# Four positions per partition for q and k, with f16 transposes by column tiles and strided queries, in a block-causal attention and expert kernel

## Chip, cores, metric

One core of one Trainium2 chip. The metric is the device time of one execution in microseconds; medians and the lowest and highest of the runs are given, over all runs, the slow ones of a kernel too (over 1.5% above its fastest); ratios use the fast ones alone. Executions of one kernel spread here (412.61 to 422.98 us for the nine runs of the kernel before on one chip), so small differences are judged by ratios with 95% intervals.

## The reference, cut to what matters

```python
B, H, S, D = 8, 8, 576, 64              # q, k, v: f32
scores = q @ k.T / sqrt(D)              # per batch and head
mask   = (pos_i // 64) >= (pos_j // 64) # causal by blocks of 64
attn   = softmax(where(mask, scores, -1e9))
x      = (attn @ v).transpose(0, 2, 1, 3).reshape(4608, 512)
# eight experts: each row of x goes to the expert that domain_id names
out[rows of e] = relu(x[rows of e] @ w1[e]) @ w2[e]    # 512 -> 1024 -> 512
```

The kernel works on 32 pairs of heads (8 batches of 4 pairs), then on the eight experts. Both halves are long; the change is in the first.

## The kernel before

The parts that matter. Staging and loads: q and k arrive as f32 with 128 consecutive positions on 128 partitions, so every run in memory is one head's 64 values, 256 B.

```python
qS = [asb.tile([128, 4, 16, D], F32, name=f"qS{i}") for i in range(2)]   # kS alike, tS for tails
def load_qk(i, b0, b1, h0=0, h1=H):
    ...
    for c in range(4):
        nc.gpsimd.dma_start(out=dst[t % 2][:, c, o, :],
                            in_=rows(src, i, b0, b1, h0, h1, c))
```

Transposes of one pair of heads, in f32, with one PSUM buffer and one copy that casts to f16:

```python
def emit_T(p):
    PT = aps.tile([128, 2, 512], F32, name="PT", tag="PT")
    QK = asb.tile([128, 2, 512], F16, name="QK", tag="QK", bufs=3)
    for s, src in enumerate((qS[t % 2], kS[t % 2])):
        for c in range(4):
            nc.tensor.transpose(out=PT[:, s, 128 * c : 128 * c + 128],
                                in_=pair_cols(src[:, c], p), identity=identf[:])
    nc.vector.tensor_copy(out=QK[:], in_=PT[:])
```

Products: the keys are the stationary operand, the queries the moving one, contiguous in QK; each of the two heads uses its own 64 rows of the array (64*128 in the views), and the two run beside each other: both 512-wide products together last 0.39 us at 47.40 us of the kernel before.

```python
def mm_qk(o, QK, c):
    for i in range(2):
        h = slice(64 * i, 64 * i + 64)
        nc.tensor.matmul(out=o[:, i], lhsT=QK[h, 1, 128 * c : 128 * c + 128],
                         rhs=QK[h, 0, 128 * c : 512], start=True, stop=True)
```

PV is the product of the attention weights with v. The order of work for pair p: group 0 (512-wide product), transposes of pair p+2, group 1 (384 + 128), the PV products of pair p-1, group 2 (256 and twelve 64-wide ones), the rest of PV. ScalarE takes the exponentials, VectorE copies out of PSUM and divides, GpSimd casts v to f16 and issues the loads.

The softmax here doesn't subtract the row's maximum and nothing guards it: scores larger than these inputs give would overflow.

## Time and profile before

| | before |
|---|---|
| time | 421.58 us median (417.69 to 422.23, 3 runs) |
| span of the profiled run | 415.3 us |
| last division of attention starts (with its reciprocal) | 189.6 us |
| first gather of the experts | 196.87 us |
| first gather to end | 218.4 us |

The page divides the span into 40 slices of 10.4 us. Each digit is a busy share in tenths, and PEclk is the clock granted to TensorE in tenths:

```profile
PE   2764841998989879881499999969979597799000
PEclk9995985789699968998589999997989899699655
```

The first 18 digits are attention. PE has holes until the fourteenth or so, and the clock falls in and after them (8.85 us busy and a mean clock of 0.57 from 60 to 80 us). Two groups of TensorE (line, engine, operation, output<-inputs, shape, count, then busy us, mean ns of one, and idle time before them with its cause):

```profile
L336 PE MATMUL ps<-QK 64*128 64x512 f16 (+3 forms) x256 | 37.5, 335 | 0.7 <-ACT ATE L341 0.7
L394 PE MATMUL po<-vS,A 128*128 128x65 f16 x640 | 36.6, 201 | 0.0
```

The mean of 335 ns mixes four widths; the 64x512 products alone have a mean of 428 ns.

### The profile page before, as it was taken

What the parts mean: (1) busy time and instruction counts of PE and PEld (TensorE: products, weight loads), DVE (VectorE), ACT (ScalarE), POOL (GpSimd) and SP (SyncE); (2) the same over time, 40 slices, a digit from 0 to 9 for tenths busy, and PEclk for the clock granted to TensorE, in tenths of its full rate; (3) what the DMA queues carried; (4) which work ended last, traced back from release to release, by engine and by line L of the source; (5) the groups of instructions that cost most, each with busy time, mean ns of one, the idle gap of its engine ahead of it and who ended that gap; (6) DMA issues with size and microseconds to landing.
All of it is one profiled execution on the core that took longest, in us unless ns stands there. A gap on an engine that the chain in (4) does not pass through costs nothing. (4 is left out here: it accounts for less than half of the span.)

```text
span 415.3 us, 6768 instructions
## 1 busy us (share of the span) xinstructions
PE 305.5 (74%) x2758; PEld 190.5 (46%) x2758; DVE 162.1 (39%) x268; ACT 140.7 (34%) x193; POOL 220.1 (53%) x253
## 2 busy tenths in 40 slices
PE   2764841998989879881499999969979597799000
PEld 1332620665666647661264656544636344365000
DVE  6641870659388746752204242222122221222000
ACT  1230730465468746790050504130503204032000
POOL 9999742875297400000787556474655755422220
PEclk9995985789699968998589999997989899699655
DMA  7799999999999991111289986949879496212120
GB/s 148 202 235 249 229 186 231 221 256 229 204 283 209 259 192 33 29 58 59 84 140 217 211 161 141 172 120 182 151 150 174 106 184 128 84 62 77 64 76 14
DMA packets 36097, 64.48 MB, mean 155 GB/s; under 512 B 9082, under 2 KB 21886, under 8 KB 36064
## 3 DMA queue, kind: packets, MB, share of 16 engines
q0 software_dynamic: 26256, 58.08, 64.1%
q1 hardware_dynamic: 7408, 5.35, 5.1%
q10 hardware_dynamic: 2400, 0.59, 0.7%
q8 instruction: 23, 0.38, 0.4%
q14 instruction: 10, 0.08, 0.1%
HBM read 67.15 MB, written 15.20 MB: 198 GB/s over the span
## 5 line engine op out<-in xcount | busy, mean ns | idle before, releaser
L341 ACT ACTIVATE A<-ps 128x1024 f16<-128x1024 f32 (+1 forms) x96 | 84.4, 883 | 86.5 <-PE ps L336 78.5
L542 ACT ACTIVATE hT<-ph 128x640 f16<-128x640 f32 x64 | 45.1, 704 | 144.3 <-PE ph L537 144.3
L556 POOL DMA_INDIRECT out_dram<-osb,tok x40 | 40.9, 1023 | 76.9 <-DMA out_dram<-osb,tok 30.1
L551 PE MATMUL po<-w2h,hT 128*128 128x512 f16 x320 | 77.0, 404 | 0.0
L512 POOL DMA_INDIRECT xg<-x_rows,tok x40 | 40.6, 1015 | 65.9 <-issue 60.2
L537 PE MATMUL ph<-xT,w1h 128*128 128x320 f16 x512 | 73.2, 304 | 0.2 <-DVE xT L526 0.2
L537 PEld LDWEIGHTS <-w1h 128*128 128x128 f16 x512 | 50.8, 99 | 22.4 <-issue 0.6
L555 DVE COPY osb<-po 128x512 f32<-128x512 f32 x40 | 27.7, 691 | 75.0 <-PE po L551 45.4
L313 DVE CAST QK<-PT 128x1024 f16<-128x1024 f32 x32 | 39.0, 1219 | 38.0 <-PE PT L310 37.2
L551 PEld LDWEIGHTS <-hT 128*128 128x128 f16 x320 | 32.9, 104 | 40.8 <-issue 8.7
L526 DVE COPY xT<-pt 128x512 f16<-128x512 f16 x40 | 16.4, 423 | 75.8 <-PE pt L523 74.9
L310 PE MATMUL PT<-identf,qS 128*128 128x128 f32 x128 | 25.6, 322 | 21.1 <-DMA qS<-in_q_dram 9.1
L310 PE MATMUL PT<-identf,kS 128*128 128x128 f32 x128 | 26.2, 321 | 19.3 <-DMA kS<-in_k_dram 19.3
L523 PE MATMUL pt<-identh,xg 128*128 128x128 f16 x160 | 17.6, 246 | 30.9 <-DMA xg<-x_rows,tok 28.9
L336 PE MATMUL ps<-QK 64*128 64x512 f16 (+3 forms) x256 | 37.5, 335 | 0.7 <-ACT ATE L341 0.7
L394 PE MATMUL po<-vS,A 128*128 128x65 f16 x640 | 36.6, 201 | 0.0
L389 PE MATMUL po<-VE,ATE 128*128 128x130 f16 x160 | 33.2, 234 | 1.8 <-DVE x L411 1.8
L394 PEld LDWEIGHTS <-A 128*128 128x128 f16 x640 | 32.1, 103 | 1.0 <-issue 1.0
L411 DVE TENSOR_TENSOR x<-po,rc 128x768 f16<-128x768 f32 x32 | 30.6, 958 | 4.0 <-DMA x_rows<-x 2.9
L310 PEld LDWEIGHTS PT<-identf,qS 128*128 128x128 f32 x128 | 15.6, 157 | 31.7 <-DVE QT L326 9.0
L136 POOL DMA_DIRECT2D w2h<-in_moe_w_dram x32 | 23.4, 752 | 10.8 <-DMA kS<-in_k_dram 7.0
L310 PEld LDWEIGHTS PT<-identf,kS 128*128 128x128 f32 x128 | 18.3, 162 | 23.0 <-DMA kS<-in_k_dram 23.0
(92 smaller groups left out, 285.6 us busy)
## 6 DMA issues: line engine op xcount, KB each, us to landing
w1h<-in_moe_w_dram POOLq DMA_DIRECT2D x32, 256.0 KB, 5.6
w2h<-in_moe_w_dram POOLq DMA_DIRECT2D x32, 256.0 KB, 6.0
vst<-in_v_dram POOLq DMA_DIRECT2D x12, 512.0 KB, 7.4
qS<-in_q_dram POOLq DMA_DIRECT2D x12, 512.0 KB, 12.3
kS<-in_k_dram POOLq DMA_DIRECT2D x12, 512.0 KB, 18.8
x_rows<-x SPq DMA_DIRECT2D x8, 512.0 KB, 8.9
vst<-in_v_dram POOLq DMA_DIRECT2D x11, 256.0 KB, 4.0
qS<-in_q_dram POOLq DMA_DIRECT2D x4, 256.0 KB, 5.1
```

Source lines behind the costliest of these rows:

```text
L310: nc.tensor.transpose(out=PT[:, s, 128 * c : 128 * c + 128], in_=pair_cols(src[:, c], p), identity=identf[:])
L313: nc.vector.tensor_copy(out=QK[:], in_=PT[:])
L336: nc.tensor.matmul(out=o[:, i], lhsT=QK[h, 1, 128 * c : 128 * c + 128], rhs=QK[h, 0, 128 * c : 512], start=True, stop=True)
L341: nc.scalar.activation(out=o, in_=i, func=AF.Exp, scale=0.125)
L389: nc.tensor.matmul(out=o[:, 1:131], lhsT=st["AE"][:, 128 * m : 128 * m + 128], rhs=VE[b % 2][:, m, hp, 1:131], start=True, stop=(m == 0))
L394: nc.tensor.matmul(out=o[:, 1 + 65 * i : 66 + 65 * i], lhsT=at_block(st, i, c, m), rhs=vS[b % 3][:, c, hp, 1 + 65 * i : 66 + 65 * i], star ...
L411: nc.vector.tensor_tensor(out=st["x"][:, :, 128 * hp : 128 * hp + 128].rearrange("p (b w) (i z) -> p b w i z", b=2, i=2), in0=pv[:, :, :, ...
L512: nc.gpsimd.indirect_dma_start(out=g[:, blk, :], out_offset=None, in_=xd, in_offset=bass.IndirectOffsetOnAxis(ap=tok[:, blk : blk + 1], ax ...
L537: nc.tensor.matmul(out=ph[:, i, 0:hw], lhsT=w1h[:, dc, 128 * fc : 128 * fc + 128], rhs=xT[:, dc, hw * i : hw * i + hw], start=(dc == 0), s ...
L542: nc.scalar.activation(out=hT[:, fc].rearrange("p (i n) -> p i n", i=2), in_=ph[:, :, 0:hw], func=AF.Relu)
L551: nc.tensor.matmul(out=po[:], lhsT=hT[:, fc, 128 * blk : 128 * blk + 128], rhs=w2h[:, fc, :], start=(fc == 0), stop=(fc == 7))
L556: nc.gpsimd.indirect_dma_start(out=out, out_offset=bass.IndirectOffsetOnAxis(ap=tok[:, blk : blk + 1], axis=0), in_=osb[:], in_offset=None ...
```

## The change

The intent: longer runs for the loads of q and k, so that they take less DMA time. Each partition takes four neighbouring positions of one head, 1 KB in one run. Two consequences follow. First, a transpose now yields the positions in the order 0, 4, 8, ... for each of four offsets, so the keys are put in order by the copy out of PSUM, while the queries stay as they are and are read with a step. Second, the f32 staging is cast to f16 by GpSimd ahead of the transposes. The two heads of a pair no longer lie side by side, so each head is transposed into its own half of the array's columns (a column tile; 128*64 in the views below). The diff, cut to its core:

```diff
-    qS = [asb.tile([128, 4, 16, D], F32, name=f"qS{i}") for i in range(2)]
+    qs = asb.tile([128, 16, 256], F32, name="qs")          # ks alike
+    qh = [asb.tile([128, H, 256], F16, name=f"qh{i}") for i in range(4)]
 ...
+        eng.dma_start(
+            out=dst[:, o, :],
+            in_=src[b0:b1, h0:h1, n0 : n0 + 512, :].rearrange(
+                "b h (p j) d -> p (b h) (j d)", j=4))
 ...
     def emit_T(p):
-        PT = aps.tile([128, 2, 512], F32, name="PT", tag="PT")
+        PT = aps.tile([128, 2, 4, 128], F16, name="PT", tag="PT", bufs=2)
-            for c in range(4):
-                nc.tensor.transpose(out=PT[:, s, 128 * c : 128 * c + 128], ...)
-        nc.vector.tensor_copy(out=QK[:], in_=PT[:])
+            for j in range(4):
+                for i in range(2):
+                    nc.tensor.transpose(
+                        out=PT[64 * i : 64 * i + 64, s, j, :],
+                        in_=src[:, 2 * hp + i, 64 * j : 64 * j + 64],
+                        identity=identh[:])
+        nc.vector.tensor_copy(
+            out=QK[:, 0].rearrange("p (j n) -> p j n", j=4), in_=PT[:, 0])
+        nc.vector.tensor_copy(
+            out=QK[:, 1].rearrange("p (n j) -> p n j", j=4),
+            in_=PT[:, 1].rearrange("p j n -> p n j"))
+    def q_cols(QK, h, n0, n1):
+        return QK[h, 0].rearrange("p (j n) -> p n j", j=4)[:, n0 // 4 : n1 // 4, :]
 ...
-                rhs=QK[h, 0, 128 * c : 512], start=True, stop=True)
+                rhs=q_cols(QK, h, 128 * c, 512), start=True, stop=True)
```

Cut: the same reading of queries in the 64-wide products, the tails in f16, casts placed among the loads, a third buffer for gathered rows, and a clamped index for the gather.

## The prediction

> **What bounds the kernel now.** I split the span by stage first, then read who waits for whom, then the timeline of one pair of heads. The span has two halves: attention to about 190 us (the last division on VectorE starts at 189.83) and the experts from the first gather at 196.87 us. The change edits the experts hardly at all, so I ask what attention is worth. In stages of 20 us (columns: stretch, length, busy PE, PEld, DVE, ACT, POOL with counts, granted clock, DMA share, GB/s):
>
> ```profile
> 60.00:80.00 20.00, 8.85 (x90) 5.58 (x92) 5.06 (x6) 3.85 (x5) 8.67 (x11) 0.57 1.11 221
> 120.00:140.00 20.00, 17.72 (x275) 13.02 (x276) 15.31 (x21) 15.11 (x21) 14.48 (x16) 1.00 1.05 238
> 160.00:180.00 20.00, 18.85 (x298) 13.83 (x296) 15.98 (x22) 16.32 (x23) 0.00 (x0) 1.00 0.10 32
> ```
>
> From 20 to 155 us the DMA share is about 1 and TensorE has holes, with the clock halved after long ones; from 160 us the inputs are in and TensorE runs through. The table of waits names the holes:
>
> ```profile
> ACT A L341 <- PE ps L336: 78.5, 41, 16.7
> DVE QK L313 <- PE PT L310: 37.2, 12, 12.7
> PEld PT L310 <- DMA kS<-in_k_dram: 23.0, 13, 4.4
> PE PT L310 <- DMA qS<-in_q_dram: 9.1, 5, 5.1
> ```
>
> The transposes wait for k and q, and everyone else waits for TensorE. So attention is bound by the DMA until 155 us and by TensorE after. In single microseconds, v alone moves at about 340 GB/s, and q and k, with the same 256 B runs, at about 220:
>
> ```profile
> 120.00:121.00 1.00, 0.28 (x3) 0.28 (x4) 0.79 (x3) 0.92 (x1) 1.00 (x2) 1.00 1.09 360
> 129.00:130.00 1.00, 1.00 (x23) 0.70 (x19) 1.00 (x1) 0.70 (x1) 0.40 (x1) 1.00 1.10 229
> ```
>
> An unhindered pair has no hole on TensorE (timeline; start, length, then the group):
>
> ```profile
> 47.40 0.39 PE L336 MATMUL ps<-QK 64*128 64x512 f16 x2
> 47.72 0.66 PE L310 MATMUL PT<-identf,qS 128*128 128x128 f32 x4
> 48.21 0.60 PE L310 MATMUL PT<-identf,kS 128*128 128x128 f32 x4
> 48.74 0.39 PE L336 MATMUL ps<-QK 64*128 64x384 f16 x4
> ...
> 49.70 0.28 PE L336 MATMUL ps<-QK 64*128 64x256 f16 x2
> ```
>
> The next pair starts at 50.69, so a pair costs 3.29 us: transposes 1.02 (47.72 to 48.74), QK products 0.32 + 0.32 + 0.22 plus 0.31 for the twelve 64-wide ones, together 1.17, and 1.10 for PV. ACT needs 2 x 1.026 + 0.597 + 0.485 = 3.13 us a pair, so it stands just behind. 32 pairs at 3.3 are 106 us; attention takes 190. Some 65 us could be had.
>
> [...]the query operand becomes strided, and the kernel before has one such matmul to test it on, the routing product (L214, 120 moving columns, 36 B apart):
>
> ```profile
> L214 PE MATMUL PT<-Hh,L x36: 377/399/405, 80.5 to 105.5; 128*128 128x120 f16 x36
> 80.53 4.11 PE L214 MATMUL PT<-Hh,L 128*128 128x120 f16 x18
> ```
>
> Eighteen start within 4.11 us: (4.11 - 0.40)/17 = 0.218 us each, or 1.8 ns a column. Contiguous f16 runs at 0.053 us for 128 columns (eight expert transposes in 0.71 us), 0.42 ns a column. [...]the clock is 1.00 when L214 starts and 0.50 in the microsecond after its end.[...]
>
> **The change part by part.**
> 1. *Loads.* q and k are 18.9 MB. At 210 to 220 GB/s they cost about 88 us of the queue. If 1 KB runs reach the rate of v, 340 GB/s, it is 55 us: 33 us of DMA time removed. v keeps its runs (9.4 MB, 28 us). The DMA share adds up to about 148 us of full work before 156 us (135 from 20 to 155, the rest earlier); x and the first weights are what remains, about 32. The total falls to about 115 us. GpSimd issues one transfer instead of four.
> 2. *GpSimd casts.* 128x1024 f32 to f16 takes 1.045 us (the v casts). Per batch four such for q and k, and a half one: about 4.8 us, 34 us for seven batches, and fewer issues free about 35 us (48.8 us for the 50 issues of q, k and tails now, against 16 of about 1 us). GpSimd is idle from 145 to 197 us now, so this lies beside other work. Staging is now single, but each load can be issued right after its cast; I laid these out with the times above and find each batch ready 4 us or more before a slow TensorE wants it.
> 3. *Transposes.* Eight f32 ones (1.02 us) become sixteen f16 ones of 128 moving columns, 0.053 each: 0.85 us in series, 0.45 if two column tiles overlap. Gain 0.2 to 0.6 us.
> 4. *Evacuation.* One 1.219 us copy becomes a contiguous f16 one (0.42, as the 128x512 expert copies) and a reordering one of 512 elements (0.68[...], as the f32 tail copy, perhaps more). About even. PT has two buffers, which removes the short waits for QT and QK (about 1.2 us a batch, 10 us in all).
> 5. *Strided queries.* A pair has 512 + 384 + 128 + 256 = 1280 columns for QK and five 64-wide products more, 1600 columns with a step of 256 B between neighbours. At 1.8 ns that is 2.9 us in place of 1.15: **plus 1.75 us a pair**, on TensorE, which sets the pace once DMA doesn't.
>
> The sum: a pair costs 3.29 - 1.17 + 2.93 - 1.02 + 0.85 = 4.9 us (4.5 if column tiles overlap). From pair 2 at about 25 us, 30 pairs at 4.5 to 4.9 are 135 to 147 us, plus 8 for L214, 3 for the tails and 2 to drain: attention ends at 173 to 185 us, not 190. The 65 us of holes go, and 50 of them come back as slow reads. Experts unchanged (the gather now clamps its index; some 10% more rows): 421 - 5 to - 17 gives **404 to 416 us**.
>
> **Rivals.** *(a) The strided read costs little.* For it: [...]the author left the queries unordered while reordering the keys.[...] Then ACT at 3.13 and TensorE at about 3.2 us a pair set the pace, with some waits for casts in the first half; attention ends at 145 to 160 us and the kernel takes 375 to 392. I give this 0.25. *(b) The clock falls too.* Per pair the array is really fed for about 1600 x 0.42 = 0.67 us plus 0.81 us of PV columns in 4.9 us, 30%; L214 at 24% lost the clock, and the last pairs at about 50% (clock 1.00 at 184 to 190 us) did not. At half clock[...] 6 us a pair, attention to 215 or 225 us, total 440 to 455. I give this 0.27. *(c) A new wait on GpSimd*: casts behind issues in one queue, with one staging buffer. [...]batch 2 can come late; worth 5 to 10 us, and only if TensorE is fast.
>
> **Range and chances.** The middle case (0.48) puts two thirds of its weight below 413 us, the 2% line. With rival a: 0.25 + 0.48 x 0.6 = 0.54 faster; 0.20 same; 0.26 slower. Middle 409 us, range 378 to 447.
>
> **What would show it.** Mean length of the 64x512 QK matmul: 428 ns now; about 1100 if step 5 holds, 430 if rival a. The pair period in the middle of attention: 4.5 to 4.9, 3.2 or 6 us. DMA share below 0.8 from 60 us on, and few waits of the transposes for loads. Clock in attention: 1.0, or 0.5 for rival b. Sixteen transposes within 0.45 to 0.9 us. First gather at 180 to 192 us. The prediction is wrong [...]if two row tiles no longer overlap when strided, or if the late casts leave new holes.

Marks show where passages are cut from the recorded text: general statements about the hardware that no trace of this case shows, and reasons that rested on them. The sum of the middle case has all its terms: 3.29 - 1.17 + 2.93 - 1.02 + 0.85 = 4.88 us, put as 4.9 us a pair (4.5 if column tiles overlap), attention to 173 to 185 us, and 404 to 416 us in all. The 2.93 rests on L214's measured 1.8 ns a column; that a rate seen at a step of 36 B holds for the queries' 256 B was the author's estimate, and so were the rate of v for 1 KB runs and the full clock for such a pair. Rival b loses the clause from which its 6 us a pair came: 4.5 us, with PV's 1.10 and the overlapping transposes' 0.45 counted once more. No trace showed such growth, so it was an estimate too (the growth measured is in the last part but one).

## The result

The changed kernel takes 452.87 us (451.20 to 454.37, 3 runs) against 421.58 us. The ratio is 1.077, with a 95% interval of 1.065 to 1.089: slower, and outside the predicted range of 378 to 447. (A ratio here is the mean time of one kernel's fast runs over that of the other's of the same rounds, so not quite the ratio of the medians quoted.) The last division of attention starts at 223.6 us instead of 189.6, and the first gather is at 229.13 instead of 196.87. From there to the end it is 220.1 us against 218.4 (of the profiled runs). So nearly all of the loss lies in attention.

The two later stages of 20 us of the prediction, of the kernel after:

```profile
120.00:140.00 20.00, 20.00 (x205) 10.92 (x202) 8.54 (x16) 10.02 (x14) 11.79 (x15) 1.00 1.04 231
160.00:180.00 20.00, 20.00 (x211) 11.48 (x207) 7.92 (x16) 9.85 (x14) 0.00 (x0) 1.00 0.01 2
```

The holes are gone: PE is busy 20.00 of 20 us. But from 120 us on it finishes 205 matmuls where the kernel before finished 275, although each pair now has 16 transposes instead of 8. The DMA is idle from 160 us on. From the table of waits (who, for whom, total us, count, longest):

```profile
DVE rc L418 <- PE po L397: 84.5, 31, 3.7
```

VectorE waits for TensorE, as ScalarE does with 75.2 us for the products. From 80 to 220 us attention is bound by TensorE alone (20.00 of 20 us busy in each stage). One pair on its timeline (start, length, then the group):

```profile
112.11 1.02 PE L341 MATMUL ps<-QK 64*128 64x512 f16 x2
113.06 0.64 PE L311 MATMUL PT<-identh,qh 128*64 128x128 f16 x8
113.48 0.64 PE L311 MATMUL PT<-identh,kh 128*64 128x128 f16 x8
114.06 1.03 PE L341 MATMUL ps<-QK 64*128 64x384 f16 x4
115.02 0.29 PE L397 MATMUL po<-VE,ATE 128*128 128x130 f16 x1
...
115.32 0.43 PE L402 MATMUL po<-vS,A 128*128 128x65 f16 x4
...
115.65 0.54 PE L402 MATMUL po<-vS,A 128*128 128x65 f16 x6
116.12 0.60 PE L341 MATMUL ps<-QK 64*128 64x256 f16 x2
```

The divisions of neighbouring pairs of one batch are 6.0 us apart (112.2, 118.2). From starts, this pair has 0.95 for the 512-wide products, 1.00 for the transposes, 0.96 for the 384- and 128-wide ones, 1.10 us for the first part of PV, and about 1.25 for the 256- and 64-wide ones. The rest of PV takes 0.78 in the pair before it (111.33 to 112.11), which has no transposes of tails after it. **PV takes 1.88 us where it took 1.10 (0.64 and 0.46 in the pair of the prediction), and nothing was changed in it.** The groups agree:

```profile
L402 PE MATMUL po<-vS,A 128*128 128x65 f16 x640 | 55.4, 248 | 0.0
...
L311 PE MATMUL PT<-identh,kh 128*64 128x128 f16 x256 | 20.5, 314 | 2.6 <-POOL kh L112 2.6
```

The row of L341 has 84.3 us and a mean of 703 ns, more than twice the 335 of before (64x512 alone: 1021 ns). The transposes last 314 ns each and wait 2.6 us in all for GpSimd's casts of k (a like row has 8.2 us for VectorE's casts of q, at the start), and those of the tails 4.1 us.

The page, though, reports full clock for the whole of attention:

```profile
PE   2879969999999999999718999897978969699300
PEclk9999999999999999999999999999896959989855
```

That row can't be read so. The trace's first clock record is at 241.7 us, after attention, and it says "full". Before the first record the page assumes full clock. A first record that changes the clock *to* full means that it was not full before, and the durations confirm it: the PV groups last 0.29, 0.43 and 0.54 us, as in the kernel before where its records say half (0.29, 0.43, 0.54 from 39.77 to 40.40 us), against 0.23, 0.28 and 0.34 us where they say full (49.06 to 49.43). The clock was at half for all of attention. The reader should take from this that the clock row is only as good as its records; an unchanged matmul is the better thermometer.

### The profile page after: what moved, and what is told of

It is laid out like the page before. It is cut to its first block, busy times and chain, and to the rows that moved or that the text cites. A ratio compares the mean times of both kernels' runs of the same rounds, so it can differ in the third digit from the quotient of the medians.

```text
span 449.2 us, 7273 instructions
## 1 busy us (share of the span) xinstructions
PE 370.9 (83%) x3014; PEld 210.1 (47%) x3014; DVE 158.3 (35%) x302; ACT 144.8 (32%) x196; POOL 220.0 (49%) x252
## 5 line engine op out<-in xcount | busy, mean ns | idle before, releaser
L347 ACT ACTIVATE A<-ps 128x1024 f16<-128x1024 f32 (+1 forms) x96 | 84.4, 881 | 117.0 <-PE ps L341 75.2
L341 PE MATMUL ps<-QK 64*128 64x512 f16 (+3 forms) x256 | 84.3, 703 | 0.0
L402 PE MATMUL po<-vS,A 128*128 128x65 f16 x640 | 55.4, 248 | 0.0
L402 PEld LDWEIGHTS <-A 128*128 128x128 f16 x640 | 49.6, 135 | 0.9 <-issue 0.9
L397 PE MATMUL po<-VE,ATE 128*128 128x130 f16 x160 | 44.9, 297 | 1.3 <-DVE x L419 1.3
L418 DVE RECIPROCAL rc<-po 128x12 f32<-128x12 f32 x32 | 7.5, 233 | 84.5 <-PE po L397 84.5
L397 PEld LDWEIGHTS <-ATE 128*128 128x128 f16 x160 | 19.3, 121 | 31.7 <-issue 31.1
L130 POOL CAST vS<-vst 128x1024 f16<-128x1024 f32 (+1 forms) x21 | 18.7, 923 | 28.1 <-PE po L402 17.5
L122 POOL DMA_DIRECT2D vst<-in_v_dram x25 | 25.3, 1024 | 8.5 <-DMA qs<-in_q_dram 8.1
L311 PEld LDWEIGHTS <-qh 128*64 128x64 f16 x256 | 12.8, 158 | 34.0 <-issue 24.9
L311 PE MATMUL PT<-identh,qh 128*64 128x128 f16 x256 | 20.4, 314 | 8.2 <-DVE qh L112 8.2
```

The lines of the kernel that those rows point to most:

```text
L311: nc.tensor.transpose(out=PT[64 * i : 64 * i + 64, s, j, :], in_=src[:, 2 * hp + i, 64 * j : 64 * j + 64], identity=identh[:])
L341: nc.tensor.matmul(out=o[:, i].rearrange("p (n j) -> p n j", j=4), lhsT=QK[h, 1, 128 * c : 128 * c + 128], rhs=q_cols(QK, h, 128 * c, 512) ...
L347: nc.scalar.activation(out=o, in_=i, func=AF.Exp, scale=0.125)
L397: nc.tensor.matmul(out=o[:, 1:131], lhsT=st["AE"][:, 128 * m : 128 * m + 128], rhs=VE[b % 2][:, m, hp, 1:131], start=True, stop=(m == 0))
L402: nc.tensor.matmul(out=o[:, 1 + 65 * i : 66 + 65 * i], lhsT=at_block(st, i, c, m), rhs=vS[b % 3][:, c, hp, 1 + 65 * i : 66 + 65 * i], star ...
```

## The experiments

Eleven kernels ran, all with correct results. Eight shared one chip and runs of the kernel before with a median of 415.11 us; double_T, strided_aligned and early_act shared another, with 418.40 us. The theory: the strided query costs 1.85 ns a column at any clock, and in addition TensorE, which waits for operands while it counts as busy, doesn't get its full clock. The main rivals: the strided read is harmless and something else is slow (casts, column tiles); or the half clock comes from the column tiles.

| kernel | median us | range | ratio to before, 95% | last division at |
|---|---|---|---|---|
| after | 452.87 | 451.20 to 454.37 | 1.077 (1.065 to 1.089) | 223.6 |
| q_ordered | 400.24 | 396.19 to 403.62 | 0.964 (0.955 to 0.973) | 170.9 |
| c0_strided | 408.08 | 406.16 to 408.64 | 0.985 (0.981 to 0.990) | 177.0 |
| before_strided | 463.24 | 452.06 to 475.58 | 1.097 (1.087 to 1.106) | 225.6 |
| full_T | 452.87 | 451.62 to 457.59 | 1.098 (1.090 to 1.106) | 218.8 |
| double_T | 440.50 | 439.43 to 441.55 | 1.059 (1.052 to 1.066) | 212.9 |
| pairs (2 runs) | 398.12 | 397.49 to 398.75 | 0.962 (0.958 to 0.967) | 168.1 |
| in_line (2 runs) | 406.64 | 404.19 to 409.10 | 0.983 (0.974 to 0.992) | 174.5 |
| before_aligned | 405.09 | 398.37 to 408.32 | 0.968 (0.957 to 0.980) | 175.5 |
| strided_aligned | 449.64 | 427.48 to 456.34 | none | 219.9 |
| ordered_aligned | 381.30 | 378.93 to 382.14 | 0.920 (0.915 to 0.925) | 154.5 |
| early_act | 378.88 | 377.04 to 382.79 | 0.909 (0.901 to 0.918) | 145.3 |

### 1. The queries put in order (q_ordered)

```diff
         nc.vector.tensor_copy(
-            out=QK[:, 0].rearrange("p (j n) -> p j n", j=4), in_=PT[:, 0])
+            out=QK[:, 0].rearrange("p (n j) -> p n j", j=4),
+            in_=PT[:, 0].rearrange("p j n -> p n j"))
     def q_cols(QK, h, n0, n1):
-        return QK[h, 0].rearrange("p (j n) -> p n j", j=4)[:, n0 // 4 : n1 // 4, :]
+        return QK[h, 0].rearrange("p (n j) -> p n j", j=4)[:, n0 // 4 : n1 // 4, :]
```

> The changed kernel, but the queries too are put in order by the PSUM copy, so that the moving operand of the QK products is contiguous. Theory (a moving read[...] costs about 1.85 ns a column, and starves the array so that the clock stays at half): the 64x512 product falls from 1021 to about 430 ns, the PV products return to full clock, a pair costs 3.2 to 3.3 us instead of 6.04, total 375 to 392 us. Rival (the half clock or the pair time come from the column-tile transposes, the casts or the new waits): a pair stays above 5 us and the total above 430.

The rest of the change stays. 400.24 us, 3.6% faster than the kernel before. Groups of the 64x512 product alone, of this kernel:

```profile
L342 PE MATMUL ps<-QK 64*128 64x512 f16 x64 | 14.4, 448 | 0.0
```

448 ns on average instead of 1021, and late pairs come every 3.0 us (divisions at 162.5 and 165.5). So the strided read, with all that hangs on it, is worth about 50 us, and the rest of the change is a gain. The expected 375 to 392 was missed. What held the first 105 us is looked into in experiments 8 and 10.

### 2. Only the 512-wide product strided (c0_strided)

Both layouts are written, a reordered one and the one of the change; only the 512-wide product reads the strided one.

```diff
+        nc.vector.tensor_copy(out=QK[:, 2].rearrange("p (n j) -> p n j", j=4),
+                              in_=PT[:, 0].rearrange("p j n -> p n j"))
-                rhs=q_cols(QK, h, 128 * c, 512), start=True, stop=True)
+                rhs=q_cols(QK, h, 128 * c, 512, c in (0,)), start=True, stop=True)
```

> Both orders of the queries are kept; only the 512-wide product of each pair reads the strided one (512 of 1600 strided columns left). Theory: this product takes about 1020 ns whatever the clock is, all the others are contiguous; the array is fed for some 1.5 of 4 us a pair, so the clock should be full: a pair 4.0 us, total 400 to 415. If this much strided reading already costs the clock: a pair about 5 us, total 430 to 440. Rival (strided reads are slow only because the clock is low): the product takes about 600 ns and the total is as q_ordered's.

The timeline of a late pair, at a recorded clock of 1.00 (the records show full clock from 128.7 to 179.9 us):

```profile
157.75 1.02 PE L346 MATMUL ps<-QK 64*128 64x512 f16 x2
158.70 0.41 PE L311 MATMUL PT<-identh,qh 128*64 128x128 f16 x8
...
159.27 0.39 PE L346 MATMUL ps<-QK 64*128 64x384 f16 x4
```

The strided product lasts 1.02 us at full clock, as it does at half clock in the changed kernel, while the contiguous 384-wide ones beside it last 0.39. So the strided rate doesn't depend on the clock: from 157.75 to the next start at 158.70 it is 0.95 us for 512 columns (the two heads run beside each other), or 1.85 ns a column. The sixteen transposes take 0.57 us from start to end of their stretch. The pair takes 3.47 us (the next one starts at 161.22), less than the 4.0 expected. One strided product a pair doesn't cost the clock here.

### 3. Only the strided read, in the kernel before (before_strided)

```diff
-        nc.vector.tensor_copy(out=QK[:], in_=PT[:])
+        nc.vector.tensor_copy(
+            out=QK[:, 0].rearrange("p (j n) -> p n j", j=4),
+            in_=PT[:, 0].rearrange("p (n j) -> p n j", j=4))
+        nc.vector.tensor_copy(out=QK[:, 1], in_=PT[:, 1])
```

and the queries read with a step as in the change.

> The kernel before, with nothing of the change but the strided query read (its PSUM copy stores the queries four-way interleaved). Theory: the 64x512 product goes from 428 to about 1020 ns, the clock stays at half in attention, a pair costs 6 us or more, and the total is 450 to 475. Rival (the strided read is harmless, the loss is in the loads, casts and transposes): total within 2% of the kernel before.

463.24 us, with a wide spread: two of the four runs are slow (470.72 and 475.58), and the ratio uses the fast ones (452.06 and 455.76). The strided read, with the copy that serves it here, makes the kernel before 9.7% slower. That the total lies within the expected 450 to 475 is chance, since the clock was expected at half and a pair at 6 us or more: the records show full clock from 117.1 to 216.1 us, and PV runs at its full-clock lengths there:

```profile
149.87 0.28 PE L403 MATMUL po<-vS,A 128*128 128x65 f16 x4
...
150.04 0.34 PE L403 MATMUL po<-vS,A 128*128 128x65 f16 x6
...
152.51 1.02 PE L342 MATMUL ps<-QK 64*128 64x512 f16 x2
153.99 0.66 PE L310 MATMUL PT<-identf,qS 128*128 128x128 f32 x4 [0.45 <-DVE QT L332]
```

Pairs come every 5.3 us. So the same strided products don't force the half clock by themselves: with eight f32 transposes of 1.02 us beside them the clock stayed full from 117 us on. This left open what holds it at half in the changed kernel. A side effect muddles the total: the copy that writes the interleaved f16 layout is slow (VectorE's groups; it writes with a step of 256 B):

```profile
L313 DVE CAST QK<-PT 128x512 f16<-128x512 f32 x32 | 78.6, 2457 | 27.3 <-PE PT L310 27.2
```

2457 ns for 512 elements, where the contiguous copy of the keys takes 898 ns; the plan of this run had not foreseen this.

### 4. Without column tiles (full_T)

The casts interleave the two heads, so that eight full-width f16 transposes do the work of sixteen column tiles. The queries stay strided.

```diff
-                for i in range(2):
-                    nc.tensor.transpose(
-                        out=PT[64 * i : 64 * i + 64, s, j, :],
-                        in_=src[:, 2 * hp + i, 64 * j : 64 * j + 64],
-                        identity=identh[:])
+                nc.tensor.transpose(
+                    out=PT[:, s, j, :],
+                    in_=src[:, hp, j].rearrange("p i d -> p (i d)"),
+                    identity=identh[:])
```

> The changed kernel, strided queries kept, but the casts put the two heads of a pair side by side, so that 8 full-array f16 transposes replace 16 column tiles. This asks what keeps the clock at half: before_strided had the same strided products and f32 transposes and ran at full clock from 117 us on. If the column tiles don't count as work for the clock: full clock comes back, PV falls from 1.84 to 1.10 us a pair, a pair 4.7 us, total 405 to 420. If the share of time in which the array is fed decides: still half clock, a pair 5.9 to 6.0 us, total 445 to 455.

452.87 us: no gain. Pairs come every 6.0 us until 192 us, as in the changed kernel, so the half clock is not due to the column tiles. In the profiled run the first clock record, again to full, is at 192.1 us, and the pairs after it show what the changed kernel would do at full clock:

```profile
201.73 1.02 PE L342 MATMUL ps<-QK 64*128 64x512 f16 x2
202.68 0.40 PE L312 MATMUL PT<-identh,qh 128*128 128x128 f16 x4
...
206.52 1.02 PE L342 MATMUL ps<-QK 64*128 64x512 f16 x2
```

4.79 us from one 512-wide product to the next (201.73 to 206.52). This falls into the 4.5 to 4.9 us that the prediction had for full clock. So the pair was sized rightly and the clock was not. (The eight transposes take 0.56 us here, the sixteen column tiles 0.57 in experiment 2.)

### 5. Every transpose twice (double_T)

The changed kernel with each transpose issued a second time into the same place: pure extra work for the engine that is the bound.

```diff
-                for i in range(2):
+                for i in (0, 1, 0, 1):
                     nc.tensor.transpose(
```

> The changed kernel with every transpose issued twice into the same place: sixteen more column-tile transposes a pair, pure extra work for TensorE (0.42 us at full clock, 0.99 at half clock) in which the array is fed without gaps. Theory (the clock follows the share of time in which the array is really fed; strided products starve it, and in the kernel before with strided queries the f32 transposes fed it enough): the clock comes back early, the pair falls from 6.04 to 5.1 to 5.4 us although there is more work, and the kernel takes 420 to 440 us, less than 452.9. Rival (the clock in attention is held down by something else, such as column tiles or chance): the pair is 6.9 to 7.1 us and the kernel takes 475 to 490 us. Between them: the clock comes back only late, 445 to 470.

440.50 us, and all four runs (439.43 to 441.55) lie below the fastest of the changed kernel (451.20), though on another chip; by ratios the intervals just touch (1.052 to 1.066 and 1.065 to 1.089). **TensorE does more and is done sooner.** The clock records come to full at 112.9 us and stay there until 208.5. The other three runs fit: the mean clock on record is 0.857 to 0.880 in all four, and 0.944 to 0.945 in the three of the changed kernel, where the stretch before the first record counts as full. Two starts of the 512-wide products, a pair apart:

```profile
195.82 1.02 PE L341 MATMUL ps<-QK 64*128 64x512 f16 x2
196.77 0.64 PE L311 MATMUL PT<-identh,qh 128*64 128x128 f16 x16
...
201.07 1.67 PE L341 MATMUL ps<-QK 64*128 64x512 f16 x4
```

5.25 us a pair, against 6.04. A stage of 20 us at a clock that is now backed by records (columns as above):

```profile
160.00:180.00 20.00, 20.00 (x304) 10.57 (x298) 8.91 (x18) 11.32 (x15) 0.00 (x0) 1.00 0.10 32
```

304 matmuls in 20 us where the changed kernel had 211, with PE at 20.00 of 20 in both; 16 a pair are the extra ones, and in pairs it is 3.8 against 3.3. The PV product has a mean of 193 ns from 160 to 185 us, against 248 in the changed kernel. So "busy" is not what the clock follows: a TensorE that is busy without a gap, but with strided matmuls at 1.85 ns a column, was kept at half clock, and more contiguous work brought the full clock back. The total is at the edge of the expected 420 to 440, since the clock came back only at 113 us.

How much contiguous work is enough stays open. An estimate counts a pair's columns at 0.42 ns, 0.67 us for the queries, plus 0.81 for PV and the transposes (column tiles as if one after the other), and divides by the length of the pair. It gives 2.33 of 6.04 us (39%) in the changed kernel at half clock, 3.18 of 5.25 (61%) in double_T, 2.50 of 5.3 (47%) in before_strided, but also 1.91 of 4.79 (40%) in full_T after its clock had come back. A single threshold doesn't follow from that. That the clock depends on where it was before would be a guess, which no run shows; strided_aligned below, where runs of one kernel differ by 6%, doesn't speak against it.

### 6. Which step is dear (pairs, in_line)

Two layouts that are permuted too, but with other steps. In pairs, two neighbouring f16 (4 B) are read, then the read jumps 512 B ahead or 508 back (the expectation below says 256 or 512). In in_line, the read never takes the neighbour (it steps 8 B and comes back), but each run of eight columns stays within 16 B.

```diff
 # pairs
+        return QK[h, 0].rearrange(
+            "p (a n r) -> p n a r", a=2, r=2)[:, n0 // 4 : n1 // 4, :, :]
 # in_line
+        return QK[h, 0].rearrange(
+            "p (m v u) -> p m u v", v=2, u=4)[:, n0 // 8 : n1 // 8, :, :]
```

In pairs, 0.93 ns a column if every jump takes the 1.85 ns of a strided column whatever is read after it, and 430 or 608 ns if two neighbours before each jump are enough for the contiguous rate; in in_line, 430 or 608 ns if steps within 16 B cost nothing.

> The changed kernel with the queries stored so that the moving read takes two neighbours (4 bytes) and then jumps 256 or 512 bytes. [...]0.93 ns a column, the 64x512 product about 640 ns, a little above its half-clock time of 608. [...]430 ns at full clock or 608 at half. If only an unbroken run is fast: 1020. Total 396 to 415 in the first two cases.

> The changed kernel with the queries permuted only within groups of eight[...]: the moving read steps by 8 bytes and back[...]. [...]the 64x512 product takes 430 ns (608 at half clock). If it is for every step that isn't to the next element: about 1020.[...] Four small copies for the queries load VectorE by some 0.4 us a pair more; total 398 to 415 in the first case, above 440 in the second.

The 64x512 products of pairs, then of in_line, from the groups of each:

```profile
L343 PE MATMUL ps<-QK 64*128 64x512 f16 x64 | 15.7, 489 | 0.0
```

```profile
L345 PE MATMUL ps<-QK 64*128 64x512 f16 x64 | 15.1, 468 | 0.2 <-ACT A L351 0.2
```

489 and 468 ns, where the ordered kernel has 448 and the strided one 1021 (the three means include stretches at half clock, where the longest is 607, 606 and 607 ns). So neither a jump nor a step was dear in itself. What was dear is a read in which every element lies far from the one before (1.85 ns a column at 256 B here, 1.8 at the 36 B of L214); two neighbours before each jump, or eight elements within 16 B, gave nearly the contiguous rate. Where between 8 and 36 B the price sets in was not tried. At a recorded full clock the two products take 0.32 us to the next start in the ordered kernel and in in_line, 0.37 in pairs and 0.95 in c0_strided. The pairs layout costs the kernel nothing that shows: 398.12 us, as the ordered one's 400.24. The in_line kernel paid elsewhere, with four copies of 474 ns for the queries on VectorE.

### 7. Where the speed of the loads comes from (before_aligned)

The trace's packet records gave a doubt about the 1 KB runs. All the packets concerned carry 4 KB. Their median duration, beside the address at which the destination starts in each partition (from the compiled programs; the pads below bear it out):

| kernel, tensor | run | start modulo 256 B | packet |
|---|---|---|---|
| before, v | 256 B | 0 | 195 ns |
| before, q and k | 256 B | 224 | 311 ns |
| after, v | 256 B | 128 | 309 ns |
| after, q and k | 1 KB | 128 | 192 ns |
| strided_aligned, ordered_aligned, q and k | 1 KB | 0 | 165 ns |

16 engines with 4096 B in 195 ns make 336 GB/s, and with 311 ns 211 GB/s: the 340 and 220 GB/s of the prediction. So the kernel before was given two pads, that put q, k and the tails on a multiple of 256 B and keep v there:

```diff
+    pad = const.tile([128, 16], F16, name="pad")       # 32 B, ahead of the staging
+    nc.vector.memset(pad[:], 0.0)
 ...
+    padv = asb.tile([128, 112], F16, name="padv")      # 224 B, ahead of vst
+    nc.vector.memset(padv[:], 0.0)
```

> The kernel before, with 32 bytes of padding ahead of the staging of q and k and 224 bytes ahead of that of v, so that all start on a multiple of 256 bytes in the partition; nothing else. Theory (the 256-byte runs of q and k were slow, 311 ns for a packet of 4 KB against 195 ns for v, only because their destination started 224 bytes past a multiple of 256): all packets take 195 ns, the loads of attention end some 30 us earlier, total 385 to 400. Rival (q and k are slow because of what else is in flight, or their addresses in HBM): packets stay at 311 and the total within 1% of the kernel before.

405.09 us, 3.2% faster with no other change (one profile, in a slow run of 407.0). The packets of q and k now take 195 ns at the median, as those of v. Stages of the kernel before, then of the aligned one:

```profile
40.00:60.00 20.00, 14.43 (x208) 10.31 (x206) 17.39 (x29) 11.71 (x16) 13.65 (x15) 0.92 1.05 214
```

```profile
40.00:60.00 20.00, 14.50 (x166) 10.00 (x166) 15.07 (x26) 9.56 (x13) 15.69 (x18) 0.76 1.04 315
```

The DMA share is the same, 1.05 and 1.04, and it moves 315 GB/s instead of 214. The total is a little above the expected 385 to 400; the stretch from 20 to 80 us still has holes at a clock of 0.59 to 0.76. The pads change only where tiles start in SBUF, so here it is the start on that side, where the data are written, that decides: 195 ns at a multiple of 256 B, 311 at 224 past one (309 for v at 128). Other starts were not tried, and why they cost time is not shown. The 1 KB runs gain from the same alignment, though less: 165 ns for 192 (experiments 8 and 9), or 397 GB/s.

### 8. The ordered queries with the pad (ordered_aligned)

q_ordered plus a pad of 128 B, so that the runs of q, k and v are all aligned.

```diff
+    pad = const.tile([128, 64], F16, name="pad")
+    nc.vector.memset(pad[:], 0.0)
```

> q_ordered with 128 bytes of padding, so that the staging of q, k, the tails and v starts on a multiple of 256 bytes. Theory: the packets of v fall from 309 to about 195 ns, the loads of batches 2 and 3 end some 6 us earlier, the wait of the tail transposes for the cast (5.5 us) shrinks, and the total is 385 to 396 us. Rival (the loads no longer bind, GpSimd's casts and their hold on VectorE do): within 1% of q_ordered, 396 to 404.

381.30 us, 8.0% faster than the kernel before, better than the expected 385 to 396, and 16% below the changed one's median. The expectation counted v's packets alone; those of q and k gained too (192 to 165 ns). Attention's last division starts at 154.5 us. What is left in the first 60 us is seen on the timeline of VectorE, and beside it of GpSimd:

```profile
51.52 4.84 DVE L210 TENSOR_TENSOR L<-iota_x,lo_h 128x1152 f16<-128x1152 f16 x1
...
58.94 0.75 DVE L210 TENSOR_TENSOR L<-iota_x,lo_h 128x1152 f16<-128x1152 f16 x1
```

```profile
51.56 2.65 POOL L132 CAST vS<-vst 128x1024 f16<-128x1024 f32 x3
...
54.64 3.17 POOL L132 CAST vS<-vst 128x1024 f16<-128x1024 f32 x3
```

The same instruction takes 4.84 us while GpSimd casts and 0.75 us while it only issues transfers. Why it takes longer is not shown; that the casts hold it up is read from this pattern (the collisions of experiment 10). This is the price of moving casts to GpSimd, which the prediction had called "beside other work".

### 9. The strided queries with the pad (strided_aligned)

The changed kernel with the same pad and nothing else.

> The changed kernel with a pad of 128 bytes a partition ahead of the staging tiles, so that v's 256 B runs land at a multiple of 256 bytes: packets of v 195 ns instead of 309, nothing else. Theory (attention is bound by TensorE at 6.04 us a pair, transfers hidden): at most the start gains, 440 to 453 us. Rival (the late v loads make holes that cost the clock): clock returns early, pairs of 4.8 us, 410 to 430.

Inconclusive. Four runs took 427.48, 446.48, 452.81 and 456.34 us. The profile fell in a slow one, with pairs of 6.0 us and no clock record before 237.3 us. One run in four was 25 us quicker. That would fit a clock that came back early, as in double_T. The mean clock on record points there too: 0.909 in that run and 0.937 to 0.941 in the other three. In full_T the run whose records begin within attention has 0.914, its other three 0.937 to 0.944. But no trace of the quick run exists, so it isn't shown.

### 10. Fewer collisions on VectorE (early_act)

ordered_aligned with the first three VE copies on ScalarE (VE is a copy of a part of v that VectorE makes once a batch), and two tail casts put ahead of the expert weights in GpSimd's queue.

```diff
-            nc.vector.tensor_copy(
+            (nc.scalar.copy if b <= 2 else nc.vector.tensor_copy)(
                 out=VE[b % 2][64 * i : 64 * i + 64, :, :, cs],
```

> The kernel with ordered queries and the pad (381.3 us), with the first three VE copies moved from VectorE to ScalarE and the tail casts of batches 2 and 3 put ahead of the expert weights in GpSimd's queue. Theory (the first 60 us are held up by VectorE, whose copies take 4.6 to 5.2 us while GpSimd casts): 372 to 379 us. Rival (the holes there come from the transfers or from GpSimd): 380 to 383.

378.88 us (377.04 to 382.79), a ratio to before of 0.909 (0.901 to 0.918) against 0.920 (0.915 to 0.925) of ordered_aligned. The intervals overlap, so the small gain isn't proven. In the profiled runs TensorE was busy 17.48 us from 40 to 60 us instead of 13.98, as the theory wants. Either version beats both kernels of the case.

## Why the prediction was wrong, point by point

- **What bounds the kernel.** Right: once the loads came in time, TensorE set the pace, and the holes went (20.00 of 20 us busy). The 65 us that could be had are not derived in the text, and rival a's own 145 to 160 us allow 30 to 45; ordered_aligned and early_act ended attention 35 and 44 us earlier than the kernel before.
- **Loads (part 1).** The gain was seen rightly, its cause wrongly. The prediction put the 220 GB/s of q and k down to nothing that it could name, and expected the rate of v from longer runs. Experiment 7 shows that alignment in SBUF alone gives it, with 256 B runs (195 ns for 311). The longer runs give it as well (192 ns), though they too are faster when aligned (165 ns); but v, which the change moved off its alignment, went from 195 to 309 ns. "v keeps its runs (28 us)" was a miss, without weight here, as the transfers were hidden.
- **GpSimd casts (part 2).** TensorE waited 6.7 us for GpSimd's casts, 4.1 for tails and 2.6 for k, within rival c's 5 to 10, although c was said to count only with a fast TensorE. What was missed is that a VectorE instruction took 4.84 us for 0.75 meanwhile (experiment 8).
- **Transposes (part 3).** Two column tiles overlap: 0.57 us for sixteen at full clock, where sixteen in a row at 0.053 are 0.85; inside the predicted 0.45 to 0.85. At half clock they took 1.00.
- **Evacuation (part 4).** Right: 422 ns contiguous and 680 ns reordering, as predicted.
- **Strided queries (part 5).** Right in size: 1.85 ns a column against the 1.8 taken from the routing product. The whole pair at full clock was measured as 4.79 us in full_T, where 4.5 to 4.9 were predicted.
- **The step that failed** is the clock in the sum of the pair: "a pair costs ... 4.9 us" and "The middle case (0.48)" took the full clock, and rival b, "The clock falls too", got 0.27. The runs showed half clock in all of attention: PV 1.88 us for 1.10, the transposes 1.00 for 0.45 to 0.85, the pair 6.04 for 4.9. An estimate from the two measured periods: 30 pairs x (6.04 - 4.79) are 37.5 us, and without them the 452.9 would be 415, inside the predicted 404 to 416. The text had the argument for rival b in hand (30% of the time fed, L214 losing the clock at 24%), and weighed the last pairs of the kernel before, at about 50%, as much. With 6.04 for 4.9 us, and routing and tails as measured (8.3 and 5.0, where it had 8 and 3), the prediction's own sum is 25 + 30 x 6.04 + 8.3 + 5.0 + 2 = 221.5 us, against 223.6 measured. Rival b said 6 us a pair, attention to 215 or 225 us, and 440 to 455 in all: the result, although PV and the transposes grew by factors of 1.7 and 1.75 (1.88 us for 1.10, 1.00 for 0.57), less than its estimate had. With 0.27 for it, an upper end at 447 was too low as well, since half of rival b's own range lay at or above that.
- **What the chances hid.** Rival a, the harmless read, got 0.25, though the trace held a measurement against it (L214), and the one reason for it that is left was the author's choice. Some of that weight belonged to b. And the experiments show what the choice cost: with ordered queries the same change is 3.6% faster, with a pad 8.0%.

What stays open: the rule by which the clock returns. Shown are that the changed kernel stays at half clock in all of attention and doesn't with ordered queries, that this is not due to column tiles, and that doubling the transposes brings the full clock back. That the clock follows the share of contiguous work is argued from these runs; a threshold is not shown, and one run of strided_aligned may have come back by chance.

## What to carry to other kernels

Put a reordering into a copy that has to be made anyway, and let a matmul's moving operand take at least two neighbouring f16 at a time: single elements 256 B apart took over four times as long (1.85 ns a column for 0.42), and may cost the clock besides, which slows the matmuls that are contiguous (PV took 1.88 us a pair for 1.10). Don't trust "TensorE is 100% busy" or the clock row: compare the length of an unchanged matmul. Before lengthening the runs of a DMA, look where its destination starts in the partition; two pads (32 and 224 B) brought the loads of the kernel before to the same rate without longer runs (195 ns for a packet of 4 KB, where it was 311 and longer runs gave 192).
